# Windowed attention and a residual MLP on one core: a written-out instruction order replaced by a list scheduler, sink values taken through TensorE

## Chip, core and metric

One core of a Trainium2 chip runs the whole program. The metric is the device time of one execution in microseconds (us), from three runs of the kernel before.

## What is computed

Attention with 4 sink keys and a window of 128 keys over 4 batches of 8 heads, 768 positions and 64 dims; its output is the input of a token-mixing and channel-mixing MLP.

```python
keep = (pos_k < 4) | ((pos_q - pos_k >= 0) & (pos_q - pos_k < 128))
a = softmax(where(keep, q @ k.T / 8, -1e9));  x = (a @ v) as (B, 768, 512)
tok = einsum('ts,bsd->btd', w_tok, alpha1 * x + beta1)
u = x + lam * tok
ch = maximum((alpha2 * u + beta2) @ w_ch1, 0) @ w_ch2      # 512 -> 2048 -> 512
out = u + lam * ch
```

## The kernel before

The 768 positions are six blocks of 128. Per batch, eight tiles of q and k (`nat`, two heads each) are loaded, cast to fp16 (`n`), transposed by six TensorE transposes into `tp` and copied to `qkT` (line 210 is the copy helper on VectorE and GpSimd, line 208 on ScalarE). `scores` (lines 257 to 284) makes a block of scores in PSUM tile `S`, and ScalarE's exp turns it into `E`; `mask` multiplies it by a band mask (in batch 0 the mask is a bias added by TensorE instead). `pv` (293 to 313) multiplies E with the values `vf`, plus the sinks' part `es` with `vs`; `norm` (315 to 332) divides into `x` and makes `xh`, alpha1 times x, with GpSimd. `vs` holds the 4 sink rows of v spread over all partitions: four loads a batch (`load_vs`, line 77), and a GpSimd multiply with the mask `bm` (`fill_vs`, line 225).

The MLP of a batch: `tok` (six groups of 6 matmuls, line 382), the residual add on VectorE (389), a ScalarE cast `u` (391), transposes `uTp` to `uT` (404, 409), `h` (32 groups of 4 matmuls, 424) with relu on ScalarE or VectorE to `hT` (432, 430), `ch` (6 tiles of 16 matmuls, 444), add (450) and store (451). Weights are loaded once: w_tok is cast with row sums (472), transposed (475) and copied; w_ch1 is cast in quarters of 1 MB (`cast_w1`), w_ch2 is multiplied by lam in quarters (`cast_w2`, 487), through two 1 MB staging buffers `wst`.

Nothing reorders at run time: each engine runs its own instructions in the order in which the Python code issues them, and all loads and stores stand in SP's queue in one order. Before, that order is written by hand: lines 494 to 566 for attention of batch 0 and its token mixing, and from 569 on a list of `slots` (the MLP of batch b) with a `side` list of steps of attention b + 1 hung between them at computed positions. The loads of q, k, v of the next batch are issued together (`prefetch`, 613). In batch 0:

```python
side[6].append(lambda nb=nb: prefetch(nb))
side[12].append(lambda: (cast_w1(3, (A, G_)), load_w2(1)))
side[23].append(lambda: (cast_w2(1, (V, G_, V, G_)), load_w2(3)))
```

Of the kernel before, what the change touches and what calls it, by code (L numbers as in the profile page):

```python
# [10 lines left out]
ALU = mybir.AluOpType  # L11


@with_exitstack
def kernel(
# [17 lines left out]
    nc = tc.nc  # L33
# [22 lines left out]


    nat_tiles = {}
    v_tiles = {}

    def load_qk(b, hp, t):
        nat = sb.tile([P, 2, NR * D], FP32, tag="nat", bufs=8, name=f"nat{b}_{hp}_{t}")
        src = (q, k)[t][b, 2 * hp : 2 * hp + 2]
        nc.sync.dma_start(nat, src.rearrange("h (p r) d -> p h (r d)", p=P))
        nat_tiles[b, hp, t] = nat

    def load_v(b, r):
        vn = sb.tile([P, H, D], FP32, tag="vnat", bufs=4, name=f"vnat{b}_{r}")
        nc.sync.dma_start(vn, v[b, :, r * P : (r + 1) * P, :].rearrange("h p d -> p h d"))
        v_tiles[b, r] = vn  # L70

    vsn = {}

    def load_vs(b):
        vsn[b] = sb.tile([P, H, D], FP32, tag="vsn", bufs=1, name=f"vsn{b}")
        for i in range(n_sink):
            nc.sync.dma_start(
                vsn[b][i::n_sink], v[b, :, i, :].unsqueeze(0).to_broadcast([P // n_sink, H, D]))

    QK_ORDER = [(hp, t) for hp in range(HP) for t in range(2)]  # L80
# [75 lines left out]
    nc.vector.memset(bm, 1.0)  # L156

    for m in (maskn, mask0):
# [20 lines left out]
    )  # L179
    bias0 = const.tile([P, 1, 2 * P], FP16, name="bias0")  # L180
# [23 lines left out]
    xh_t = {}

    def copy(eng, o, i):
        if eng is nc.scalar:
            eng.copy(o, i)
        else:
            eng.tensor_copy(o, i)  # L210

    def cast_qk(b, hp, t, eng):
        nat = nat_tiles.pop((b, hp, t))
        d = sb.tile([P, NR, P], FP16, tag="n16", bufs=4, name=f"n16_{b}_{hp}_{t}")
        copy(eng, d.rearrange("p r (e d) -> p e r d", e=2), nat.rearrange("p e (r d) -> p e r d", r=NR))
        n16[b, hp, t] = d

    def cast_v(b, r, eng):
        copy(eng, vf[r][:, :, 0:D], v_tiles.pop((b, r)))

    def cast_v0(G, r, eng):
        copy(eng, vf[r][:, 4 * G : 4 * G + 4, 0:D], v0[G][:, r])

    def fill_vs(b):
        nc.gpsimd.tensor_mul(vs[b % 2][:, :, 0:D], vsn.pop(b), bmf.to_broadcast([P, H, D]))

    def trans(b, hp, t, eng=None):
        if b not in qkT:
            qkT[b] = sb.tile([P, 2 * HP, S], FP16, tag="qkT", bufs=1, name=f"qkT{b}")
        src = n16.pop((b, hp, t))  # L230
        pt = ps.tile([P, S], FP16, tag="d", bufs=3, name=f"tp{b}_{hp}_{t}")
        o = qkT[b][:, 2 * hp + t, :]
        for r in range(NR):
            nc.tensor.transpose(pt[:, r * P : (r + 1) * P], src[:, r, :], iden)  # L234
        copy(eng or nc.vector, o.rearrange("p (i r) -> p i r", r=NR),
             pt.rearrange("p (r i) -> p i r", r=NR))

    def sinks(b, Gs=(0, 1)):
# [3 lines left out]
        for e in range(2):  # L242
            nc.vector.tensor_copy(
                ks[64 * e : 64 * e + 64, hs, e * n_sink : (e + 1) * n_sink],
                qkT[b].rearrange("p (a t) s -> p a t s", t=2)[64 * e : 64 * e + 64, hs, 1, 0:n_sink],
            )
        pt = ps.tile([P, S - 2 * P], FP32, tag="d", bufs=3, name=f"sk{b}_{Gs[0]}")
        for hp in range(hs.start, hs.stop):
            nc.tensor.matmul(
                pt[32 * hp : 32 * hp + 32, :], ks[:, hp, :], qkT[b][:, 2 * hp, 2 * P : S],  # L250
                start=True, stop=True,
            )
# [410 lines left out]
```

## Time and profile before

| | us |
|---|---|
| median of 3 runs (range) | 337.0 (335.55 to 338.72) |
| profiled execution | 335.56 |
| its span, first to last instruction | 333.8 |
| PE busy, share of the span | 275.8, 83% |
| VectorE (DVE), ScalarE (ACT), GpSimd (POOL) busy | 167.0, 113.9, 118.8 |

PE is TensorE's matmul, PEld its weight load, SPq the queue in which SP issues DMAs. PEclk is TensorE's granted clock, 1.0 for 2.4 GHz and 0.5 for 1.2 GHz. Matmuls overlap and their ends are modelled, so a busy PE is not one at its peak. The span and the profiled execution's time differ by 1.8 us.

### The profile page before, as it was taken

What the parts mean: (1) busy time and instruction counts of PE and PEld (TensorE: products, weight loads), DVE (VectorE), ACT (ScalarE), POOL (GpSimd) and SP (SyncE); (2) the same over time, 40 slices, a digit from 0 to 9 for tenths busy, and PEclk for the clock granted to TensorE, in tenths of its full rate; (3) what the DMA queues carried; (4) which work ended last, traced back from release to release, by engine and by line L of the source; (5) the groups of instructions that cost most, each with busy time, mean ns of one, the idle gap of its engine ahead of it and who ended that gap; (6) DMA issues with size and microseconds to landing.
All of it is one profiled execution on the core that took longest, in us unless ns stands there. A gap on an engine that the chain in (4) does not pass through costs nothing.

```text
span 333.8 us, 4946 instructions
## 1 busy us (share of the span) xinstructions
PE 275.8 (83%) x1980; PEld 145.0 (43%) x1980; DVE 167.0 (50%) x325; ACT 113.9 (34%) x182; POOL 118.8 (36%) x138
## 2 busy tenths in 40 slices
PE   1775565789805888899999999999999999999995
PEld 1341222445403334445645455455554454566442
DVE  3362243552608887638836453388373634632211
ACT  3536313157200444103377420132765101445000
POOL 4484251002609936574403534453035350000000
PEclk9999567699975999999999999999999999999999
DMA  7899503037996205972000029940000111000021
GB/s 225 239 256 358 150 3 126 0 84 274 353 262 212 45 32 171 312 213 64 2 0 2 0 85 340 229 136 0 2 2 1 64 65 63 2 0 0 33 93 64
DMA packets 48166, 38.06 MB, mean 114 GB/s; under 512 B 31632, under 2 KB 39824, under 8 KB 48144
## 3 DMA queue, kind: packets, MB, share of 16 engines
q1 hardware_dynamic: 48144, 37.76, 36.8%
q8 instruction: 15, 0.25, 0.3%
q14 instruction: 7, 0.06, 0.1%
HBM read 31.46 MB, written 6.29 MB: 113 GB/s over the span
## 4 chain that ended last, share of the span: by engine, by line
PE 56%; DVE 20%; issue 8%; ACT 5%; POOL 5%; SPq 3%; DMA 2%; DVEq 0%; POOLq 0%; ACTq 0%
PE ch L444 22%; PE h L424 15%; PE tok L382 7%; DVE qkT L210 5%; DVE x L389 3%; DVE E L289 3%; PE S L271 3%; DVE uT L409 2%; DVE x L323 2%; POOL n L210 2%; ACT E L278 2%; ACT wt L472 2%; DMA wst_w<-in_moe_w_ch_dram 2%; SPq L96 2%; PE pv L310 1%
## 5 line engine op out<-in xcount | busy, mean ns | idle before, releaser
L424 PE MATMUL h<-uT,w1f 128*128 128x384 f16 x512 | 94.1, 330 | 2.7 <-ACT hT L432 1.4
L444 PE MATMUL ch<-w2f,hT 128*128 128x512 f16 x384 | 89.0, 379 | 0.0
L424 PEld LDWEIGHTS <-w1f 128*128 128x128 f16 x512 | 48.0, 99 | 35.6 <-issue 8.0
L432 ACT ACTIVATE hT<-h 128x384 f16<-128x384 f32 x88 | 42.7, 493 | 60.3 <-PE h L424 59.3
L444 PEld LDWEIGHTS <-hT 128*128 128x128 f16 x384 | 35.1, 98 | 38.4 <-issue 1.3
L278 ACT ACTIVATE E<-S 128x1024 f16<-128x1024 f32 (+1 forms) x42 | 40.4, 1003 | 29.0 <-PE S L271 29.0
L331 POOL TENSOR_TENSOR tmp<-x,la_b 128x512 f32<-128x512 f32 x18 | 22.8, 1269 | 74.4 <-DVE x L323 74.4
L391 ACT CAST u<-x 128x512 f16<-128x512 f32 x24 | 14.9, 620 | 82.4 <-DVE x L389 79.4
L430 DVE TENSOR_SCALAR hT<-h 128x384 f16<-128x384 f32 x40 | 22.2, 556 | 41.1 <-PE h L424 41.1
L450 DVE TENSOR_TENSOR x<-x,ch 128x512 f32<-128x512 f32 x24 | 16.5, 687 | 46.7 <-PE ch L444 46.7
L234 PE MATMUL tp<-iden,n 128*128 128x128 f16 x192 | 18.3, 239 | 24.7 <-POOL n L210 16.9
L382 PE MATMUL tok<-xh,wtokT 128*128 128x512 f16 x144 | 36.7, 409 | 0.7 <-DVE uT L409 0.6
L210 DVE COPY qkT<-tp 128x768 f16<-128x768 f16 x30 | 28.4, 953 | 10.5 <-PE tp L234 10.4
L210 POOL CAST n<-nat 128x768 f16<-128x768 f32 x29 | 24.4, 859 | 19.0 <-issue 12.9
L234 PEld LDWEIGHTS <-n 128*128 128x128 f16 x192 | 14.2, 107 | 31.4 <-POOL n L210 18.9
L332 POOL TENSOR_TENSOR xh<-tmp,lb_b 128x512 f16<-128x512 f32 x18 | 23.5, 1305 | 1.4
L382 PEld LDWEIGHTS <-wtokT 128*128 128x128 f16 x144 | 14.5, 104 | 18.0 <-issue 3.6
L389 DVE TENSOR_TENSOR x<-x,tok 128x512 f32<-128x512 f32 x24 | 16.5, 688 | 10.8 <-PE tok L382 10.2
L323 DVE TENSOR_TENSOR x<-pv,rec 128x256 f32<-128x256 f32 x48 | 20.4, 425 | 1.7
L289 DVE TENSOR_TENSOR E<-E,maskn 128x1024 f16<-128x1024 f16 x24 | 18.5, 772 | 1.4 <-ACT E L278 1.4
L487 POOL TENSOR_TENSOR w2f<-wst_w,lam_b 128x512 f16<-128x512 f32 x8 | 11.8, 1496 | 15.4 <-DMA wst_w<-in_moe_w_ch_dram 15.4
L306 PE MATMUL pv<-vf,E 128*128 128x65 f16 x160 | 15.7, 197 | 1.5 <-DVE x L323 1.2
(64 smaller groups left out, 226.1 us busy)
## 6 DMA issues: line engine op xcount, KB each, us to landing
wst_w<-in_moe_w_ch_dram SPq DMA_DIRECT2D x8, 1024.0 KB, 5.5
nat<-in_q_dram SPq DMA_DIRECT2D x16, 384.0 KB, 6.2
nat<-in_k_dram SPq DMA_DIRECT2D x16, 384.0 KB, 6.7
out_dram<-x SPq DMA_DIRECT2D x24, 256.0 KB, 2.0
vnat<-in_v_dram SPq DMA_DIRECT2D x18, 256.0 KB, 6.2
wtn<-in_moe_w_tok_dram SPq DMA_DIRECT2D x6, 384.0 KB, 7.6
v<-in_v_dram SPq DMA_DIRECT2D x12, 128.0 KB, 6.1
vsn<-in_v_dram SPq DMA_DIRECT2D x16, 64.0 KB, 3.1
```

The lines of the kernel that those rows point to most:

```text
L210: eng.tensor_copy(o, i)
L234: nc.tensor.transpose(pt[:, r * P : (r + 1) * P], src[:, r, :], iden)
L278: nc.scalar.activation(eT, pS, AF.Exp, scale=scale)
L289: nc.vector.tensor_mul(ev, ev, m.to_broadcast(list(ev.shape)))
L323: nc.vector.tensor_mul(x[:, 4 * G : 4 * G + 4, :], po[:, :, 0:D], rec.to_broadcast([P, 4, D]))
L331: nc.gpsimd.tensor_mul(tmp, xf, la1_b)
L332: nc.gpsimd.tensor_add(xh_t[b, r], tmp, lb1_b)
L382: nc.tensor.matmul(pt, wtokT[:, si, ti * P : (ti + 1) * P], xh_t[b, si], start=(si == 0), stop=(si == NR - 1),)
L389: nc.vector.tensor_add(xf, xf, pt)
L424: nc.tensor.matmul(ph, w1f[:, c, fi * P : (fi + 1) * P], uT[0][:, c, chk * NTOK : (chk + 1) * NTOK], start=(c == 0), stop=(c == NC - 1),)
L432: nc.scalar.activation(hT[chk][:, fi, :], ph, AF.Relu)
L444: nc.tensor.matmul(pch[ti], hT[chk][:, fi, nt * P : (nt + 1) * P], w2f[:, fi, :], start=(fi == 0), stop=(fi == NF - 1),)
```

## The change

The order is no longer written by hand. Each step becomes a task with a priority, the engines that may run it with a guessed cost in ns, the tasks it needs and the buffers it uses. `emit` repeatedly takes the task that can start first by its own bookkeeping (ties by priority), chooses the engine, hands it a buffer and issues it. The order is fixed when the kernel is built.

```diff
+    def emit(self):
...
+        while done < len(self.tasks):
+            best = None
+            for r, t in open_:
+                at = t.ready
...
+                for e in t.engs:
+                    key = (max(free[e], at), r, free[e] + t.engs[e])
+                    if best is None or key < best[0]:
+                        best = (key, t, e)
...
+            if e == SP:
+                channel = max(channel, free[e] + 1500.0) + t.lands
+                t.seen = channel + 300.0
+            else:
+                t.seen = free[e] + SEEN[e]
...
-    def fill_vs(b):
-        nc.gpsimd.tensor_mul(vs[b % 2][:, :, 0:D], vsn.pop(b), bmf.to_broadcast([P, H, D]))
+        def mm(e):
+            nc.tensor.matmul(pt.t, sel, vf[0][:, :, 0:D], start=True, stop=True)
+
+        def ev(e):
+            nc.vector.tensor_mul(vs[:, :, 0:D], pt.t, bmf.to_broadcast([P, H, D]))
...
+            done["xh", b, r, G] = add(p + 8.2, {POOL: 730, DVE: 420}, half, [a, done["la1"]], [bx, bh])
...
+            done["w1", i, c] = add(
+                p, {ACT: 600, POOL: 645, DVE: 330},
...
+            done["w2", 4 * i + a] = add(
+                p, {DVE: 900, POOL: 1400},
...
+        done["h", b, chk, fi] = add(p + 0.1, {ACT: 493, DVE: 556}, relu, [a], [ph, bh])
...
+    nc.scalar.dma_start(alpha2_c, moe_alpha2.rearrange("(c p) -> p c", p=P))
+    nc.scalar.dma_start(beta2_c, moe_beta2.rearrange("(c p) -> p c", p=P))
...
+        for i in range(4):
+            load_w2(at(), i)
...
+            pl = w0 - (0 if b == 0 else 30)
+            for i, (hp, t) in enumerate(QK_ORDER):
+                load_qk(pl + 0.5 * i, nb, hp, t)
```

- Sink rows: the 16 loads are gone. `sel`, a 128x128 fp16 matrix of ones and zeros made at the start, picks the first 4 rows of `vf` in one 512-column matmul per batch, and VectorE multiplies PSUM by `bm`. There is one `vs` buffer where there were two.
- PSUM: `pv` had a bank of its own and all else three; now all share four.
- The loads of alpha2 and beta2 (512 elements each) go from SP's queue to the front of ScalarE's.
- Casts of w_ch1 are four per quarter instead of two, on any of three engines; products of w_ch2 go to VectorE or GpSimd as `emit` finds them; so do the relus of h (ScalarE or VectorE) and batch 0's halves of xh.
- Two `ch` tiles are now filled in turns, 4 matmuls each.

ScalarE, from the end of attention of batch 0 to the token mixing (`E0` exp, `wt16` cast of w_tok, `u16` cast after tok). Before:

```order
L278 ACTIVATE E0_5_1_541<-S0_5_1_534 128x512
L472 ACTIVATE wt16_2_543,rs_71<-wtn0_109 128x768
L208 CAST w1f_165<-wst_w1_0_113 128x2x512
L391 CAST u16_0_0_597<-x0_0_244 128x512
L472 ACTIVATE wt16_3_599,rs_71<-wtn1_115 128x768
L391 CAST u16_0_1_618<-x0_1_270 128x512
L472 ACTIVATE wt16_4_620,rs_71<-wtn1_115 128x768
L391 CAST u16_0_2_639<-x0_2_306 128x512
L472 ACTIVATE wt16_5_641,rs_71<-wtn1_115 128x768
```

And now:

```order
L461 ACTIVATE E0_5_1_592<-S0_5_1_565 128x512
L563 ACTIVATE wt16_3_612,rs_71<-wtn1_263 128x768
L563 ACTIVATE wt16_4_626,rs_71<-wtn1_263 128x768
L204 COPY wtokT_119<-wT3_628 128x6x128
L204 COPY wtokT_119<-wT4_644 128x6x128
L563 ACTIVATE wt16_5_674,rs_71<-wtn1_263 128x768
L204 COPY wtokT_119<-wT5_690 128x6x128
L204 CAST u16_0_0_715<-x0_0_246 128x512
L204 CAST u16_0_1_728<-x0_1_299 128x512
```

The casts 3 to 5 of w_tok stood behind the casts of u that follow a tok; they now stand ahead of all of them.

SP's queue around the second quarter of w_ch2 (`wst_w2_1`; the digit in `nat1`, `vnat2` is the batch). Before:

```order
L64 DMA nat1_3_1_787<-in_k_dram 128x2x384
L69 DMA vnat1_0_789<-in_v_dram 128x8x64
L69 DMA vnat1_1_791<-in_v_dram 128x8x64
L69 DMA vnat1_2_793<-in_v_dram 128x8x64
L69 DMA vnat1_3_795<-in_v_dram 128x8x64
L77 DMA vsn1_797<-in_v_dram 32x8x64 x4
L110 DMA wst_w2_1_840<-in_moe_w_ch2_dram 128x4x512
```

And now:

```order
L331 DMA wst_w1_3_753<-in_moe_w_ch1_dram 128x4x512
L300 DMA vnat1_4_758<-in_v_dram 128x8x64
L300 DMA vnat1_5_775<-in_v_dram 128x8x64
L300 DMA vnat2_0_789<-in_v_dram 128x8x64
L300 DMA vnat2_1_808<-in_v_dram 128x8x64
L294 DMA nat2_3_1_819<-in_k_dram 128x2x384
L331 DMA wst_w2_0_857<-in_moe_w_ch2_dram 128x4x512
L294 DMA nat3_0_0_868<-in_q_dram 128x2x384
L294 DMA nat3_0_1_950<-in_k_dram 128x2x384
L294 DMA nat3_1_0_962<-in_q_dram 128x2x384
L331 DMA wst_w2_1_982<-in_moe_w_ch2_dram 128x4x512
```

Before, the eight loads of q and k of batch 1 and these of v stood between w2_0 and w2_1. Now they stand ahead of most weights, and loads of batches 2 and 3 stand among the quarters.

VectorE around the products of w_ch2 (`w2f`) in batch 0. Before:

```order
L210 COPY qkT1_908<-tp1_0_1_925 128x768
L430 TENSOR_SCALAR hT0_1_750<-h0_1_11_933 128x384
L487 TENSOR_TENSOR w2f_166<-wst_w2_1_840,lam_b_66 128x512 x2
L210 COPY qkT1_908<-tp1_1_0_947 128x768
L210 COPY qkT1_908<-tp1_1_1_966 128x768
L210 COPY qkT1_908<-tp1_2_0_985 128x768
```

And now:

```order
L470 TENSOR_TENSOR E1_0_1_1040<-E1_0_1_1040,mask0_79 128x1024
L417 TENSOR_TENSOR vs_117<-vsp1_1038,bm_85 128x8x64
L591 TENSOR_TENSOR w2f_121<-wst_w2_0_857,lam_b_66 128x512 x2
L470 TENSOR_TENSOR E1_1_0_1072<-E1_1_0_1072,maskn_80 128x1024
L470 TENSOR_TENSOR E1_1_1_1082<-E1_1_1_1082,maskn_80 128x1024
L516 RECIPROCAL rec1_0_0_1130<-pv1_0_0_1084 128x4
```

The products of w2_1 stood ahead of six of the eight qkT copies of batch 1; all eight now come before the first product, and the products stand between the masks.

## Rows read from the trace of the kernel before

**Rows 1.** TensorE's granted clock in 40 equal slices of the span

```profile
PEclk9999567699975999999999999999999999999999
```

**Rows 2.** Windows by stage: us, busy time of each engine, PEclk, DMA share, GB/s

```profile
25.70:45.10 19.40, 11.36 (x108) 5.47 (x108) 5.56 (x17) 9.61 (x14) 6.11 (x11) 0.72 0.61 205
45.10:68.40 23.30, 14.75 (x70) 6.81 (x68) 11.63 (x20) 5.05 (x11) 5.42 (x5) 0.72 0.12 45
68.40:92.00 23.60, 20.39 (x141) 12.13 (x139) 11.31 (x18) 12.30 (x23) 7.54 (x7) 1.00 0.81 253
92.00:114.80 22.80, 9.14 (x61) 5.46 (x62) 12.31 (x15) 2.99 (x6) 15.04 (x16) 0.70 0.67 188
114.80:146.90 32.10, 28.46 (x234) 13.33 (x233) 22.30 (x42) 10.32 (x12) 19.65 (x17) 1.00 0.55 166
212.90:278.80 65.90, 63.23 (x481) 34.01 (x480) 37.40 (x75) 24.77 (x40) 22.91 (x23) 1.00 0.17 52
278.80:333.80 55.00, 51.10 (x285) 26.64 (x282) 17.73 (x31) 14.31 (x28) 0.00 (x0) 1.00 0.09 34
```

**Rows 3.** Timeline of one round of token mixing, batch 0: start, us, engine, line

```profile
55.79 0.62 ACT L391 CAST u<-x 128x512 f16<-128x512 f32 x1 [4.00 <-DVE x L389]
56.32 0.84 ACT L472 ACTIVATE wt<-wtn 128x768 f16<-128x768 f32 x1
...
57.30 0.51 PE L475 MATMUL wT<-iden,wt 128*128 128x128 f16 x6 [2.27 <-ACT wt L472]
57.65 2.30 PE L382 MATMUL tok<-xh,wtokT 128*128 128x512 f16 x6
...
61.23 0.84 ACT L472 ACTIVATE wt<-wtn 128x768 f16<-128x768 f32 x1
```

**Rows 4.** Timeline, 80 to 105 us: SP's queue, then GpSimd, VectorE, TensorE

```profile
83.09 7.80 SPq L69 DMA_DIRECT2D vnat<-in_v_dram  x4
...
94.17 9.41 SPq L110 DMA_DIRECT2D wst_w<-in_moe_w_ch_dram  x3
...
82.13 2.49 POOL L487 TENSOR_TENSOR w2f<-wst_w,lam_b 128x512 f16<-128x512 f32 x2 [4.25 <-DMA wst_w<-in_moe_w_ch_dram]
...
99.76 3.43 POOL L487 TENSOR_TENSOR w2f<-wst_w,lam_b 128x512 f16<-128x512 f32 x2 [11.13 <-DMA wst_w<-in_moe_w_ch_dram]
...
99.71 2.36 DVE L487 TENSOR_TENSOR w2f<-wst_w,lam_b 128x512 f16<-128x512 f32 x2 [9.88 <-DMA wst_w<-in_moe_w_ch_dram]
...
104.01 0.82 PE L234 MATMUL tp<-iden,n 128*128 128x128 f16 x6 [12.40 <-POOL n L210]
```

**Rows 5.** Chain that ended last, its two longest pieces: start, us, what

```profile
291.66 17.70 PE h L424 x108
309.36 20.73 PE ch L444 x96
```

**Rows 6.** Groups by line: xcount | busy us, mean ns | idle before

```profile
L278 ACT ACTIVATE E<-S 128x1024 f16<-128x1024 f32 x40 | 39.2, 1023 | 25.1 <-PE S L271 25.1
...
L332 POOL TENSOR_TENSOR xh<-tmp,lb_b 128x512 f16<-128x512 f32 x18 | 23.5, 1305 | 1.4
...
L289 DVE TENSOR_TENSOR E<-E,maskn 128x1024 f16<-128x1024 f16 x24 | 18.5, 772 | 1.4 <-ACT E L278 1.4
...
L487 POOL TENSOR_TENSOR w2f<-wst_w,lam_b 128x512 f16<-128x512 f32 x8 | 11.8, 1496 | 15.4 <-DMA wst_w<-in_moe_w_ch_dram 15.4
...
L210 POOL CAST vf<-vnat 128x512 f16<-128x512 f32 x18 | 11.3, 643 | 0.0
L487 DVE TENSOR_TENSOR w2f<-wst_w,lam_b 128x512 f16<-128x512 f32 x8 | 9.9, 1279 | 9.9 <-DMA wst_w<-in_moe_w_ch_dram 9.9
```

**Rows 7.** Timeline of the start, SP's queue and ScalarE

```profile
9.34 3.44 SPq L77 DMA_DIRECT2D vsn<-in_v_dram  x4
...
5.05 0.83 ACT L208 CAST n<-nat 128x768 f16<-128x768 f32 x1 [2.97 <-DMA nat<-in_k_dram]
```

**Rows 8.** Window of 2 us in the loads of q and k, columns as in rows 2

```profile
84.00:86.00 2.00, 1.93 (x16) 1.04 (x15) 1.86 (x3) 0.49 (x1) 2.00 (x3) 1.00 1.07 400
```

More of the change, by code (lines that the diff above doesn't have):

```diff
@@ L1 @@
+import bisect
 from contextlib import ExitStack
@@ L11, with __init__ @@
 ALU = mybir.AluOpType
+PE, ACT, DVE, POOL, SP = "pe", "act", "dve", "pool", "sp"
+SEEN = {PE: 200, ACT: 60, DVE: 60, POOL: 70}
+class Buf:
+    def __init__(self, kind, shape, dtype, name):
+        self.kind, self.shape, self.dtype, self.name = kind, shape, dtype, name
+        self.left = 0
+        self.freed = 0.0
+        self.home = None
+        self.t = None
+class Task:
+    def __init__(self, prio, engs, fn, after, uses, mode, lands):
+        self.prio, self.engs, self.fn, self.uses = prio, engs, fn, uses
+        self.mode, self.lands = mode, lands
+        self.needs = [a for a in after if a is not None and a.seen is None]
+        self.ready = max([0.0] + [a.seen for a in after if a is not None and a.seen is not None])
+        self.then = []
+        self.seen = None
@@ L55, with copy @@
     ctx.enter_context(tc.manual_schedule())
[L58 to L80, printed above, removed]
+    engine = {ACT: nc.scalar, DVE: nc.vector, POOL: nc.gpsimd}
+    pools = {
+        "nat": (sb, [P, 2, NR * D], FP32),
+        "vnat": (sb, [P, H, D], FP32),
+        "n16": (sb, [P, NR, P], FP16),
+        "qkT": (sb, [P, 2 * HP, S], FP16),
+        "E": (sb, [P, 2, 2, 2 * P], FP16),
+        "es": (sb, [P, S - 2 * P], FP16),
+        "x": (sb, [P, H, D], FP32),
+        "xh": (sb, [P, DM], FP16),
+        "tmp": (sb, [P, DM], FP32),
+        "rec": (sb, [P, 4, 1], FP32),
+        "u16": (sb, [P, DM], FP16),
+        "uT": (sb, [P, NC, S], FP16),
+        "hT": (sb, [P, NF, NTOK], FP16),
+        "wst": (sb, [P, 4, 512], FP32),
+        "d": (ps, [P, 512], FP32),
+        "S": (ps, [P, 2, 512], FP32),
+    }
+    homes = {
+        "nat": 8, "vnat": 4, "n16": 4, "qkT": 1, "E": 6, "es": 1, "x": 12, "xh": 6, "tmp": 2,
+        "rec": 2, "u16": 4, "uT": 1, "hT": 2, "wst": 2, "d": 4, "S": 2,
+    }
+    plan = Plan(pools, homes)
+    add = plan.add
+    def copy(e, o, i):
+        if e == ACT:
+            nc.scalar.copy(o, i)
+        else:
+            engine[e].tensor_copy(o, i)
     lam_b = const.tile([P, DM], FP32, name="lam_b")
@@ L156 @@
     nc.vector.memset(bm, 1.0)
-    for m in (maskn, mask0):
+    sel = const.tile([P, P], FP16, name="sel")
+    nc.vector.memset(sel, 0.0)
+    for m in (mask0, maskn):
         nc.gpsimd.affine_select(
@@ L239, in sinks @@
+    def sinks(p, b, Gs=(0, 1)):
         n = len(Gs)
@@ L241, in sinks @@
         g = slice(64 * Gs[0], 64 * Gs[0] + 64 * n)
[L242 to L252, printed above, removed]
@@ new lines, in mlp2, with mm, oa @@
+    def mlp2(p, b, ti, part):
+        chk, nt = ti // 3, ti % 3
+        if part == 0:
+            pch[b, ti] = Buf("d", None, None, f"ch{b}_{ti}")
+        pc, bh, bx = pch[b, ti], hT[b, chk], x[b, ti]
+        fis = range(4 * part, 4 * part + 4)
+        def mm(e):
+            for fi in fis:
+                nc.tensor.matmul(
+                    pc.t, bh.t[:, fi, nt * P : (nt + 1) * P], w2f[:, fi, :],
+                    start=(fi == 0), stop=(fi == NF - 1))
+        a = done["ch", b, ti] = add(
+            p, {PE: 4 * 214}, mm,
+            [done["h", b, chk, fi] for fi in fis] + [done["w2", fi] for fi in fis]
+            + [done.get(("ch", b, ti))], [pc, bh])
+        if part == 3:
+            def oa(e):
+                xf = bx.t.rearrange("p h d -> p (h d)")
+                nc.vector.tensor_add(xf, xf, pc.t)
+            a = add(p + 0.1, {DVE: 690}, oa, [a, done["u16", b, ti]], [pc, bx])
+            add(p + 0.2, {SP: 480}, lambda e: nc.sync.dma_start(
+                out[b, ti * P : (ti + 1) * P, :], bx.t.rearrange("p h d -> p (h d)")),
+                [a], [bx], lands=800)
@@ new lines, with at @@
+    t0 = -1000.0
+    n = 0
+    def at():
+        nonlocal n
+        n += 1
+        return t0 + 0.5 * n
+    for hp, t in QK_ORDER[:4]:
+        load_qk(at(), 0, hp, t)
+    for r in range(2):
+        load_v0(at(), 0, r)
+    load_const(at(), "lam", lam_b, moe_lam)
+    load_const(at(), "a1", la1_b, moe_alpha1)
+    for r in range(2, NR):
+        load_v0(at(), 0, r)
+    for hp, t in QK_ORDER[4:]:
+        load_qk(at(), 0, hp, t)
+    for r in range(NR):
+        load_v0(at(), 1, r)
+    for ti in range(3):
+        load_wtok(at(), ti)
@@ new lines @@
+    for i, (hp, t) in enumerate(QK_ORDER):
+        g = -950 + 5 * i if i < 4 else -890 + 8 * (i - 4)
+        trans(g, 0, hp, t, ANY, {DVE: 955, ACT: 880}, cast_p=g - 20)
+    for G in range(2):
+        for r in range(NR):
+            cast_v0(-900 + 60 * G + 10 * r, G, r)
+    fill_vs(-890, 0)
+    for G in range(2):
+        base = -900 + 60 * G
+        for j in range(NR):
+            scores(base + 10 * j, 0, j, (G,), bias=True)
+            if j == 1:
+                sinks(base + 12, 0, (G,))
+        for r in range(NR):
+            pv(base + 10 * r + 14, 0, r, G)
@@ L456, in dense @@
+    for ti in range(NR):
+        cast_wtok(-800 + 8 * ti, ti)
+    cast_w1(-770, 0)
+    STEP = 100.0
+    for b in range(B):
+        w0 = STEP * b
         if b == 0:
+            seq = [("tok", ti) for ti in range(3)] + [("uT", 0, 0), ("uT", 0, 1)]
+            seq += [("tok", ti) for ti in range(3, NR)]
             m1 = []
@@ L561 @@
[L561 to L581 removed]
+                    m1 += [("m1", chk, fi) for fi in range(4 * qd, 4 * qd + 4)]
@@ new lines @@
+            m1.insert(3, ("uT", 1, 0))
+            m1.insert(5, ("uT", 1, 1))
+        else:
+            seq = [("tok", ti) for ti in range(5)] + [("uT", 0, 0), ("uT", 0, 1), ("tok", 5)]
+            m1 = [("m1", 0, fi) for fi in range(NF)]
+            m1.insert(4, ("uT", 1, 0))
+            m1.insert(6, ("uT", 1, 1))
+            m1 += [("m1", 1, fi) for fi in range(NF)]
+        seq += m1
+        seq += [("m2", ti, part) for ti in range(NR) for part in range(4)]
+        ns = len(seq)
+        if b == 0:
+            for i in range(1, 4):
+                cast_w1(w0 + 8 + 8 * (i - 1) - 4, i)
+            for i in range(4):
+                cast_w2(w0 + 26 + 4 * i, i)
```

817 lines of the change are left out of this document (420 added, 397 removed).

## Prediction

> **What bounds the kernel now.** I read the slices first, then windows cut at the stages, then the timeline inside the windows where TensorE is idle, and the groups by line last, for prices. The slices show TensorE at 2.4 GHz throughout the second half, and below it in two places in the first [rows 1]. The windows say why the halves differ [rows 2]. The last batch has no attention beside it and takes 55.0 us, 51.1 of them TensorE. A batch with the next one's attention beside it takes 65.9, of which TensorE is idle for 2.7. Batch 0 has no such rhythm: token mixing of batch 1 starts only at 146.9. Of the 66.3 us from 25.7 to 92 TensorE shows 46.5 busy, most of it at a mean clock of 0.72, and from 92 to 114.8 only 9.1 of 22.8. So this is a TensorE-bound kernel behind a front that is bound by waits, and the change has to earn its time in the front.
>
> Two kinds of wait are in that front. In token mixing each round is a loop over three engines: ScalarE casts u of the last tile, then casts a row of w_tok, TensorE transposes it after 2.27 us without a matmul, and only then comes the next tok [rows 3]. The casts of two rounds start at 56.32 and 61.23, so a round takes 4.9 us, for six matmuls. From 92 on, VectorE and GpSimd both sit at the product with the second quarter of w_ch2, for 9.88 and 11.13 us; its load was issued at 94.17, behind four loads of v that took SP's queue 7.80 us; and TensorE waits 12.40 us for a cast of n that stands behind GpSimd's product [rows 4].
>
> **The change part by part.** The sum is made against the profiled execution, 335.56, which is its span of 333.8 and 1.76 around it, and lies 1.4 under the median of the three runs.
>
> Start to the end of attention, batch 0. The four sink loads held SP's queue for 3.44 us at 9.34 [rows 7]; all loads behind them come that much earlier. The alpha2 and beta2 issues go ahead of ScalarE's first cast, which waited 2.97 us for its own load [rows 7]: I count nothing, and at most 2 us if two issues outlast that cover; the two short ops that make `sel` stand before GpSimd's first load in the same way. Before, the second half of the heads starts at 25.7 and token mixing at 45.1, and ScalarE is busy for 9.6 of these 19.4 us [rows 2], because each cast of w_tok, its transposes and the next scores wait for one another in turn. The new order gives ScalarE more: six exps (one of them half as long), one of the sinks (half), five w_tok casts (0.84 and the read of a row sum, 1.0) and four copies of the same shape (0.84), together 6 x 1.02 + 5 x 1.0 + 4 x 0.84 = 14.5 [rows 3, 6], with gaps 15, now without waiting in turn. It starts at about 23 (the first w_tok cast now stands ahead of the first of these exps and waits for its load, which eats half of the 3.4 us won). 23 + 15 = 38 for the start of token mixing, 7 us earlier. GpSimd's halves of xh end there too. One wait is new: the matmul with `sel` needs the first block of v for all heads, and pv of blocks 2 to 5 stand behind it on TensorE; that load is issued behind only four tiles of q and k (1 us each, [rows 8]) more than before's sink rows were, so I count nothing, at most 2.
>
> Token mixing, 45.1 to 68.4 before. The loop is cut: the casts of w_tok stand ahead of every cast of u. Left are 36 matmuls of 512 columns. The dense run of ch prices one at 20.73 / 96 = 0.216 us [rows 5], so 7.8 us at 2.4 GHz; as the stage before leaves TensorE half idle, I take the first two tiles at 1.2 GHz (+2.6), and 1.6 for the transposes. 38 + 12 = 50 for the first h; before it was 68.4. Lower bound 10, upper 18 (the clock low throughout, 16 + 2).
>
> h with attention of batch 1, 68.4 to 114.8 before: 46.4 us. h itself is 128 x 17.70 / 108 = 21.0 us [rows 5]. The eight tiles of transposes, five of six score blocks and some pv lie between, about 27,000 columns for a whole attention, three quarters of them here, at 0.216 per 512: 8.5 us. So 30, and 80 for the first ch. The 12.40 us go only if no load is late. Since w_ch2's quarters now stand behind loads of three batches, I follow the queue. At 400 GB/s [rows 8] a q or k tile takes 1.0 us and a quarter 2.6; v's 256-byte pieces are slower, between that and the 134 GB/s of 1 MB in 7.80 us behind a backlog [rows 4]; I take 270. Up to w1_1 the queue holds 13 MB by the tiles' sizes, which land by 43 at a mean 300; four of v and w1_2 by 50; seven of q and k, w1_3, four of v, one of k and w2_0 by 68; three more and w2_1 by 74; w2_2 by 80. VectorE wants w2_0 at about 72. These all come in time, by 3 to 5 us. w2_3 does not: its buffer is w2_1's, whose last product on GpSimd stands behind the first tmp of batch 1, so it is issued near 84, lands at 88 and is multiplied by 93, where TensorE wants it at 88. A stall of 5.
>
> ch with the rest of attention, 114.8 to 146.9 before: 32.1. Now 24 groups of 4 at 0.864 are 20.7, pv and scores 4, the stall 5: 30, which ends at 110. GpSimd agrees: from 69 on it has eight products of w_ch2 less those VectorE takes in both orders (8 x 1.496 stay), six pairs of tmp and xh (12 x 1.3) and six v casts (6 x 0.643), 31.4 us in all [rows 6], and most waits of it lie inside: 100 at the earliest, about 108 with them.
>
> Here the profile gives a lever against the change, since it adds VectorE work with two SBUF operands beside a GpSimd that is full. GpSimd's two products took 2.49 us with little beside them, and 3.43 beside VectorE's two, which took 2.36 [rows 4]: it lost 0.94, not 2.36. My 1.496 includes this. The Trainium skill (SBUF — State Buffer, section "SBUF: two separate sides") says that the pair of ports they share is an exclusive lock and the other engine blocks for the whole instruction. By that rule every mask and product of VectorE would stop GpSimd. The trace shows less than half of it.
>
> Steady batches, 65.9 each. TensorE's work hardly changes: four matmuls of 512 columns in all are added, 0.9 us. Visible idle is 2.7 [rows 2]; by columns the floor is 51.1 + 27,000 / 512 x 0.216 = 62.5, and 60.2 if score matmuls on the two halves of the rows overlap fully. New orders of tp, pv and ch can remove idle, and cannot remove columns. I take 63.6; bounds 60.2 and 67, one us above today: two ch tiles filled in turns hold two of the four shared PSUM banks, and a pv that finds none free stops the matmuls behind it until a norm. Sinks leave GpSimd; VectorE gets four products of 128x512, at most 1.279 each as for the same shape [rows 6], and it is busy for 37 of 66: nothing on the path.
>
> Last batch: same matmuls, same last add and store: 55.0.
>
> Sum: 110 + 2 x 63.6 + 55.0 = 292.2, and 1.8 around it, 294.0; with the 1.4 to the median, 295.
>
> **The rivals.** (1) Weights come late and replace the removed wait. For it: loads of batches 2 and 3 stand between the quarters, each waiting for a buffer that a cast must free, and casts wait for transposes. Against it: before, SP's queue waited on hand-placed issues, not on bytes. If w2_3's products end at 108, not 93: 295 + 15 = 310. (2) All goes well: no stall at w2_3 and no late load (104), batches at 60.5: 295 - 6 - 6 = 283. (3) VectorE and GpSimd exclude each other: ten masks of 0.772 and eight products of 1.279 [rows 6] fall into GpSimd's 31 us; that is 18, of which 1.496 holds about half, and of the other 9 a third finds GpSimd waiting anyway: 6 more, 301. This is the rule of the Trainium skill named above. (4) Slower: TensorE never gets its clock back in the front. The rows show it at 0.5 to 0.75 after thin stretches [rows 1, 2]. If scattered short waits kept it at 1.2 GHz from 38 to the end of ch, the 7.8 + 21 + 20.7 + 11 us of matmuls there would take twice as long, 60.5 more less the 2.6 counted already and the 5 of stall that it hides: 110 + 53 = 163 for batch 1, 348 in all. It decides from 41 us of doubled work on. Against it: from 68.4 to 92, with h alone, it was 1.00 [rows 2], and the new front is denser. (5) The change doesn't do what it says: the order rests on guessed costs, and the in-order queues give back as other waits what they save; the front stays at 147: 337.
>
> **How the numbers follow.** Forecast 0.58, (1) 0.16, (2) 0.10, (3) 0.10, (4) 0.04, (5) 0.02. The forecast's own error is some 8 us, from the stage bounds. The range runs from just under (2) to just past (1): 281 to 312. A run of this kernel scatters by about 1%, so faster means below 333.6 and slower above 340.4. Only (4) is slower, 0.04, and (5) the same, 0.02: faster has 0.94.
>
> **What would show it.** In the changed profile: the first tok near 38, the first h near 50, the first ch near 80, tok of batch 1 near 110; no wait of TensorE above 6 us after 30; a clock of 1.0 from about 45 on; then two batches of 63 to 64 and one of 55. A wait of VectorE or GpSimd on a `wst_w` load of over 8 us speaks for (1); GpSimd's tmp and xh well above 1.3 for (3); a low clock with TensorE busy for (4). The forecast is wrong if tok of batch 1 comes after 125, or if a steady batch takes more than 67.

## The result and the profile after

The changed kernel takes 292.33 us (median of 4 runs, 291.89 to 293.79) against 337.86 for the kernel before on the same chip: a ratio of 0.867, 95% interval 0.860 to 0.873, so 13% faster. 295.0 was predicted. The clock row and the windows of the profile after, cut at its own stages (attention of batch 0 with the transposes of w_tok; token mixing; h; ch; the two steady batches; the last batch), answer to [rows 1] and [rows 2], with the same columns:

```profile
PEclk9999789999799899999999999999999999999999
```

```profile
0.00:39.10 39.10, 25.78 (x269) 14.54 (x270) 26.58 (x68) 24.58 (x36) 22.69 (x39) 0.91 1.01 315
39.10:48.70 9.60, 9.60 (x70) 5.25 (x68) 8.63 (x14) 5.13 (x10) 7.76 (x12) 1.00 0.97 254
48.70:82.70 34.00, 28.83 (x231) 16.91 (x229) 25.01 (x38) 19.63 (x35) 16.38 (x16) 0.95 1.04 324
82.70:111.70 29.00, 25.31 (x174) 12.17 (x173) 20.86 (x35) 3.73 (x5) 25.87 (x21) 0.94 0.44 125
111.70:173.60 61.90, 61.62 (x482) 34.41 (x481) 37.99 (x76) 25.57 (x41) 25.89 (x26) 1.00 0.19 61
173.60:235.50 61.90, 61.62 (x482) 34.47 (x481) 37.97 (x76) 25.57 (x41) 19.04 (x16) 1.00 0.07 27
235.50:291.10 55.60, 51.78 (x289) 27.07 (x287) 20.45 (x37) 11.96 (x23) 0.00 (x0) 1.00 0.10 38
```

Batch 1's token mixing starts at 111.7 instead of 146.9: 35 of the 43 us that the span lost. The other 8 are two steady batches of 61.9 instead of 65.9, in which TensorE's visible idle time fell from 2.7 to 0.3 us. The last batch takes 0.6 more.

The DMA share (the last but one number) is about 1.0 up to 82.7, where [rows 2] had 0.12 to 0.81: the transfers now fill the front. That share alone doesn't say that they bind it (the start of a_pvbank, below, has 1.01 too and is 8.3 us longer), but the chain that ended last has loads in it, in pieces of seven to eleven microseconds (start, us, what):

```profile
22.28 11.37 DMA nat<-in_q_dram
33.73 10.04 DMA wst_w<-in_moe_w_ch_dram
44.60 7.21 DMA wst_w<-in_moe_w_ch_dram
...
64.08 7.43 DMA wst_w<-in_moe_w_ch_dram
```

The timeline of the place that [rows 4] showed before, w_ch2's arrival (start, us, engine, line, operation, and in brackets the idle time before it and what ended it):

```profile
52.92 9.90 SPq L300 DMA_DIRECT2D vnat<-in_v_dram  x4
...
64.08 0.37 SPq L331 DMA_DIRECT2D wst_w<-in_moe_w_ch_dram  x1
...
71.58 3.44 POOL L591 TENSOR_TENSOR w2f<-wst_w,lam_b 128x512 f16<-128x512 f32 x2 [6.53 <-DMA wst_w<-in_moe_w_ch_dram]
...
77.19 0.68 DVE L470 TENSOR_TENSOR E<-E,maskn 128x1024 f16<-128x1024 f16 x1
...
85.06 2.89 DVE L591 TENSOR_TENSOR w2f<-wst_w,lam_b 128x512 f16<-128x512 f32 x2
...
85.68 6.73 POOL L591 TENSOR_TENSOR w2f<-wst_w,lam_b 128x512 f16<-128x512 f32 x4
...
87.87 1.75 DVE L470 TENSOR_TENSOR E<-E,maskn 128x1024 f16<-128x1024 f16 x1
...
89.55 3.42 DVE L591 TENSOR_TENSOR w2f<-wst_w,lam_b 128x512 f16<-128x512 f32 x2
...
93.57 4.43 PE L693 MATMUL ch<-w2f,hT 128*128 128x512 f16 x12 [3.20 <-DVE x L517]
```

GpSimd still waits 6.53 us for the first quarter, issued at 64.08, after four v loads that held the queue for 9.90. From 77.3 to 93.6 VectorE is busy for 15.8 of 16.3 us and GpSimd for 16.2, and a norm that would free a PSUM buffer comes behind VectorE's products: TensorE waits 3.20 us for it. The 12.40 us wait is gone.

### The profile page after: what moved, and what is told of

Same layout as the page of the kernel before. It is cut to its first block, busy times and chain, and to the rows that moved or that the text cites. A ratio compares the mean times of both kernels' runs of the same rounds, so it can differ in the third digit from the quotient of the medians.

```text
span 291.1 us, 4977 instructions
## 1 busy us (share of the span) xinstructions
PE 264.5 (91%) x1984; PEld 144.8 (50%) x1984; DVE 177.5 (61%) x338; ACT 116.2 (40%) x189; POOL 117.6 (40%) x127
## 3 DMA queue, kind: packets, MB, share of 16 engines
q1 hardware_dynamic: 42736, 36.71, 40.2%
q10 hardware_dynamic: 1056, 0.00, 0.2%
## 4 chain that ended last, share of the span: by engine, by line
PE 66%; DMA 15%; DVE 11%; SPq 4%; issue 1%; POOL 1%; ACT 0%; ACTq 0%; DVEq 0%; POOLq 0%
PE ch L693 27%; PE h L669 25%; DMA wst_w<-in_moe_w_ch_dram 8%; PE tok L608 6%; DMA nat<-in_q_dram 4%; DVE w2f L591 4%; SPq L311 3%; PE pv L493 2%; DVE E L470 2%; PE S L448 2%; DMA beta_c<-in_moe_beta_dram 2%; SPq L294 1%; DMA v<-in_v_dram 1%; PE tp L367 1%; DVE qkT L206 1%; DVE uT L654 1%
## 5 line engine op out<-in xcount | busy, mean ns | idle before, releaser
L669 PE MATMUL h<-uT,w1f 128*128 128x384 f16 x512 | 92.9, 329 | 4.4 <-DVE x L517 3.0
L693 PE MATMUL ch<-w2f,hT 128*128 128x512 f16 x384 | 90.1, 384 | 3.7 <-DVE x L517 3.2
L693 PEld LDWEIGHTS <-hT 128*128 128x128 f16 x384 | 36.1, 99 | 45.2 <-DVE x L517 3.7
L534 POOL TENSOR_TENSOR tmp<-x,la_b 128x512 f32<-128x512 f32 x18 | 24.4, 1356 | 44.8 <-DVE x L517 44.5
L608 PE MATMUL tok<-xh,wtokT 128*128 128x512 f16 x144 | 33.7, 379 | 0.0
L206 DVE COPY qkT<-tp 128x768 f16<-128x768 f16 x28 | 26.6, 951 | 2.4 <-PE tp L367 2.3
L537 POOL TENSOR_TENSOR xh<-tmp,lb_b 128x512 f16<-128x512 f32 x18 | 24.7, 1374 | 0.9
L470 DVE TENSOR_TENSOR E<-E,maskn 128x1024 f16<-128x1024 f16 x24 | 21.9, 918 | 4.5 <-ACT E L461 4.5
L493 PEld LDWEIGHTS <-E 128*128 128x128 f16 x328 | 16.3, 99 | 9.0 <-issue 2.9
L493 PE MATMUL pv<-vf,E 128*128 128x65 f16 x328 | 19.0, 196 | 1.3 <-ACT E L461 1.3
```

The source lines that it names most:

```text
L206: engine[e].tensor_copy(o, i)
L470: nc.vector.tensor_mul(ev, ev, m.to_broadcast(list(ev.shape)))
L493: nc.tensor.matmul(po.t[:, hl, :], eT.t[:, e_, off + i, c : c + P], vf[j][:, h, :], start=(r < 2 and n == 0), stop=(n == len(parts) - 1 an ...
L534: nc.gpsimd.tensor_mul(tmp.t, bx.t.rearrange("p h d -> p (h d)"), la1_b)
L537: nc.gpsimd.tensor_add(bh.t, tmp.t, lb1_b)
L608: nc.tensor.matmul(pt.t, wtokT[:, si, ti * P : (ti + 1) * P], hs[si].t, start=(si == 0), stop=(si == NR - 1))
```

## The experiments

The kernel before was timed beside each run (337.3 to 337.5). Stage starts are the starts of the first tok, h and ch on TensorE.

**One part alone, in the order by hand.** b_sinks takes only the sinks through TensorE:

```diff
-        nc.gpsimd.tensor_mul(vs[b % 2][:, :, 0:D], vsn.pop(b), bmf.to_broadcast([P, H, D]))
+        nc.tensor.matmul(pt[:, hs], sel, vf[0][:, hs, 0:D], start=True, stop=True)
+        nc.vector.tensor_mul(vs[b % 2][:, hs, 0:D], pt[:, hs], bmf[:, hs].to_broadcast([P, n, D]))
```

> The kernel before with its hand-written order; only the sink values are taken through TensorE (a matmul with the selection matrix and a VectorE product; for batch 0 once per half of the heads) and the 16 sink loads are gone. Theory (order, not sinks, makes the gain): 2 to 5 us off 337.9, because SP's queue loses 3.44 us of issues per batch, of which only those between 84 and 105 us stand in front of something that is waited for. Rival (the small sink loads were what clogged the queue): 12 us or more off, with the first tok of batch 1 at 135 or earlier instead of 146.8.

334.97 us, ratio 0.992 (0.988 to 0.996): 2.6 us, as the theory had it. TensorE still waits 11.5 us for the cast of n behind the second quarter's product.

b_loop moves three calls:

```diff
     pvn0(4, 1)
+    cast_wtok(3, V)
     pvn0(5, 1)
+    cast_wtok(4, V)
+    cast_wtok(5, V)
...
     tok[0]()
-    cast_wtok(3, V)
     tok[1]()
-    cast_wtok(4, V)
     tok[2]()
-    cast_wtok(5, V)
```

> The kernel before; only the casts and transposes of the last three rows of w_tok are moved ahead of the first tok, so that no cast of u stands in front of one. Theory (the loop over ScalarE, TensorE and VectorE sets token mixing): from the first tok to the first h 13 us instead of 23.3, some 2 to 3 us later start of tok, and the whole 6 to 9 us shorter. Rival (TensorE's half clock sets that stage, whatever the order): the stage stays above 19 us and the gain is under 3.

328.15 us, ratio 0.973 (0.967 to 0.979), 9.1 us less. Its window of token mixing is 15.0 long where [rows 2] had 23.3, and it starts 0.7 us earlier, not 2 to 3 later. The clock is still 0.77 (0.72 before), so the cut loop made most of the 8.3 us:

```profile
44.40:59.40 15.00, 11.90 (x52) 5.30 (x50) 10.39 (x17) 2.80 (x5) 5.14 (x5) 0.77 0.20 70
```

b_queue issues v and the sinks of batch 1 behind the second quarter of w_ch2:

```diff
-                for r in range(4):
-                    load_v(bb, r)
-                load_vs(bb)
+                if bb > 1:
+                    prefetch_v(bb)
...
+                side[12].append(lambda nb=nb: prefetch_v(nb))
```

> The kernel before; only the loads of v and of the sinks for batch 1 are issued after the second quarter of w_ch2 instead of ahead of it (the tiles of q and k stay where they are). Theory (the order in SP's queue makes the 12.40 us wait of TensorE): the waits of 9.88 and 11.13 us on that quarter shrink below 3, the whole is 7 to 11 us shorter. Rival (too many bytes, whatever their order): the wait moves to the cast of v or to the third quarter and the gain is under 3 us.

333.25 us, ratio 0.989 (0.983 to 0.994): 3.9 us, between the two. The waits are a third to a half of [rows 4], not below 3: the order was half of it. What is left I put down to bytes, which no run here tests by itself. The quarter is issued at 84.69 rather than 94.17, but lands only at 94; the eight tiles of q and k (3.1 MB) are issued just ahead of it, and from 84 to 94 the DMA engines move 391 GB/s.

```profile
84.69 0.37 SPq L110 DMA_DIRECT2D wst_w<-in_moe_w_ch_dram  x1
...
86.06 1.93 DVE L487 TENSOR_TENSOR w2f<-wst_w,lam_b 128x512 f16<-128x512 f32 x2
...
94.20 3.43 POOL L487 TENSOR_TENSOR w2f<-wst_w,lam_b 128x512 f16<-128x512 f32 x2 [3.99 <-DMA wst_w<-in_moe_w_ch_dram]
...
98.46 0.82 PE L234 MATMUL tp<-iden,n 128*128 128x128 f16 x6 [5.98 <-POOL n L210]
```

b_all has all three edits.

> The three edits of the other runs together, by hand, on the kernel before. Theory: they add up, 16 to 24 us off, with tok of batch 1 at 122 to 130; what is then missing to 292.3 (20 to 28 us) lies in the start (6), in the h and ch stage of batch 0 beside the attention of batch 1 (6 to 10), and in the two steady batches (4 each). Rival (only an order that is packed as a whole gets the gain, since each wait removed by hand comes back as the next one): under 12 us.

322.95 us, ratio 0.958 (0.954 to 0.963). By the ratios the three parts nearly add up (15.6 us one by one, 14.0 together), so the rival falls, but so does the size that was expected, and tok of batch 1 starts at 134.8. Span against span, 31.2 us are missing to the changed kernel: 9.1 until the first tok (48.2 against 39.1), 5.3 in token mixing, 6.1 in h, 2.6 in ch, 8.5 in the steady batches, less 0.4 in the last.

**One part taken out of the changed kernel.** a_sinkloads brings the loads back:

```diff
-            nc.tensor.matmul(pt.t, sel, vf[0][:, :, 0:D], start=True, stop=True)
+                nc.sync.dma_start(
+                    bf.t[i::n_sink], v[b, :, i, :].unsqueeze(0).to_broadcast([P // n_sink, H, D]))
```

> The changed kernel with the sink values loaded again (four loads per batch, GpSimd's product into vs) and planned by the same scheduler. Theory (the order makes the gain): 1 to 4 us above 292.3, from 3.44 us more of SP's queue in the start and one GpSimd product more per batch where GpSimd is full, 25.9 of the 29.0 us from 82.7 to 111.7. Rival (the sinks through TensorE carry a good part of the gain in this packed order): 8 us or more above.

296.99 us, ratio 0.880 (0.876 to 0.883): 4.7 us above, just past the theory's end. The first tok comes 3.1 us later, about the queue's 3.44, and tok of batch 1 6.7 later. In the order by hand the same part was worth 2.6; that a front full of loads feels SP's queue more is my reading, which no run isolates.

a_fixed binds every step to the engine that it had before:

```diff
-                p, {DVE: 900, POOL: 1400},
+                p, {POOL: 1400} if a % 2 else {DVE: 900},
-        done["h", b, chk, fi] = add(p + 0.1, {ACT: 493, DVE: 556}, relu, [a], [ph, bh])
+        done["h", b, chk, fi] = add(p + 0.1, {DVE: 556} if fi % 3 == 2 else {ACT: 493}, relu, [a], [ph, bh])
```

> The changed kernel without the elastic choice of engine: each cast, copy, half of xh, relu and product of weights is bound to the engine that it had before; order, buffers and sinks as the scheduler makes them. Theory (order, not choice of engine): 0 to 5 us above 292.3, all of it ahead of batch 1. Rival (the choice of engine carries the front): 10 us or more above, with the first tok at 44 or later.

294.38 us, ratio 0.871 (0.867 to 0.875), whose interval overlaps that of the changed kernel. So the choice of engine is worth at most a few microseconds. They are not where I expected them: tok of batch 1 starts at 111.9, as with the choice, and the steady batches take 62.5 instead of 61.9.

a_ab puts alpha2 and beta2 back into SP's queue, behind w_tok:

```diff
-    nc.scalar.dma_start(alpha2_c, moe_alpha2.rearrange("(c p) -> p c", p=P))
-    nc.scalar.dma_start(beta2_c, moe_beta2.rearrange("(c p) -> p c", p=P))
...
+        done[nm] = add(at(), {SP: 500}, lambda e, tl=tl, ap=ap: nc.sync.dma_start(
+            tl, ap.rearrange("(c p) -> p c", p=P)), lands=800)
```

> The changed kernel with the loads of alpha2 and beta2 back in SP's queue, behind the rows of w_tok. Prediction's step (they cost nothing where they are, since ScalarE waits for its first tile anyway): within 0.5 us of 292.3, the first tok at 39. Theory now (their 1024 four-byte packets delay the first tiles; ScalarE's first cast began at 6.28, not at 5.05, and TensorE at 5.32, not at 4.56): 0.8 to 1.5 us less, the first tok at 38.

292.2 us, ratio 0.865 (0.861 to 0.868): no difference, so the second theory falls for the whole. The first microseconds do move. TensorE's first transposes, of the changed kernel and then of a_ab, each with ScalarE's first cast:

```profile
5.32 0.82 PE L367 MATMUL tp<-iden,n 128*128 128x128 f16 x6 [5.32 <-DVE n L206]
...
6.28 0.83 ACT L204 CAST n<-nat 128x768 f16<-128x768 f32 x1 [3.12 <-DMA nat<-in_k_dram]
```

```profile
4.46 0.82 PE L365 MATMUL tp<-iden,n 128*128 128x128 f16 x6 [4.46 <-DVE n L206]
...
5.02 0.83 ACT L204 CAST n<-nat 128x768 f16<-128x768 f32 x1 [2.94 <-DMA nat<-in_k_dram]
```

The first tok, though, came at 40.2 in a_ab and 39.1 in the changed kernel; the 0.86 us don't reach it.

a_pvbank divides PSUM as before:

```diff
-        "rec": 2, "u16": 4, "uT": 1, "hT": 2, "wst": 2, "d": 4, "S": 2,
+        "rec": 2, "u16": 4, "uT": 1, "hT": 2, "wst": 2, "d": 3, "pv": 1, "S": 2,
```

> The changed kernel with PSUM divided as before: three shared buffers, and one of its own for pv, so that the planner can't give pv's bank to h, tok or the transposes, nor two banks to pv. Theory (the 4 us that a steady batch gained, 65.9 to 61.9, come from the pooled fourth bank): 64 to 66 us for each of the two steady batches, 4 to 10 us above 292.3 in all. Rival (they come from the order alone): batches at 62 to 63, within 2 us of 292.3.

300.69 us, ratio 0.890 (0.886 to 0.894): 8.4 above, a size that the theory gave, at a place that it did not. The windows of the start and of the steady batches:

```profile
0.00:47.40 47.40, 29.43 (x275) 16.29 (x276) 30.11 (x75) 25.05 (x37) 27.92 (x44) 0.87 1.01 299
...
120.10:180.30 60.20, 59.46 (x447) 32.20 (x447) 36.41 (x73) 24.69 (x39) 24.32 (x24) 1.00 0.17 55
180.30:244.00 63.70, 62.85 (x483) 34.39 (x482) 40.66 (x79) 24.20 (x38) 18.52 (x16) 1.00 0.07 26
```

The steady batches take 62.0 on the mean, as with the pooled bank, so what they won isn't the bank's. The start takes 8.3 more. The edit also makes the scheduler plan another order, so the 8.3 are the worth of the bank with the order that it allows. TensorE's waits from 20 to 48 us name two places (in total, times, longest): pv, with one bank, waits 4.8 for norms, and the transposes of w_tok wait 4.5 for a VectorE copy, which I read as the one that empties one of the three shared banks.

```profile
PE wT L570 <- DVE qkT L207: 4.5, 1, 4.5
PE pv L494 <- DVE x L518: 3.4, 2, 2.5
PE pv L487 <- DVE x L518: 1.4, 2, 0.7
```

The changed kernel has neither wait there; its longest up to the first tok is:

```profile
PE tp L367 <- POOL n L206: 3.1, 1, 3.1
```

**What holds the front now.** Either the order of the loads or the weight products: two theories, each with an edit. a_w2act lightens the products on VectorE and GpSimd (w_ch2 and lam are rounded to fp16 ahead of the product too, not only behind it):

```diff
-            done["w2", 4 * i + a] = add(
-                p, {DVE: 900, POOL: 1400},
-                lambda e, a=a: engine[e].tensor_mul(w2f[:, 4 * i + a, :], src.t[:, a, :], lam_b),
+            c = add(p, {ACT: 620}, lambda e, a=a: nc.scalar.copy(w2f[:, 4 * i + a, :], src.t[:, a, :]),
...
+                lambda e, a=a: nc.vector.tensor_mul(w2f[:, 4 * i + a, :], w2f[:, 4 * i + a, :], lam16),
```

> The changed kernel, in which w_ch2 is cast to fp16 by ScalarE and then multiplied by an fp16 copy of lam in place on VectorE, so that GpSimd has no product of weights and VectorE's have two bytes an element. Theory (from 72 to 97 us VectorE and GpSimd, both full with these products in fp32 beside each other, set the pace of TensorE, and GpSimd again to 111.7): 4 to 9 us below 292.3, with the first ch at 76 to 81 and tok of batch 1 at 103 to 108. Rival (the loads of the quarters, or the PSUM buffers and ScalarE's relus, set it): within 2 us, or slower, because ScalarE gets 16 casts of 0.62 us.

289.0 us, ratio 0.856 (0.853 to 0.860), 3.3 less, under the theory's 4. ch takes 24.7 instead of 29.0 and h 33.0 instead of 34.0: most of the gain lies in ch.

a_late loads batches 2 and 3 behind the weights; the new dependency serves the planner alone, so only the order changes:

```diff
+        late = [done["wst", "w2_3"]] if b > 1 else []
...
-            uses=[bf], lands=1030)
+            late, uses=[bf], lands=1030)
```

> The changed kernel, in which the loads of q, k and v of batches 2 and 3 are planned after the load of the last quarter of w_ch2 (before, eight tiles of batch 2 stood ahead of the last quarter of w_ch1 in SP's queue and eleven of batches 2 and 3 between that and the second quarter of w_ch2). Theory A (bytes loaded too soon delay the weights: GpSimd waited 6.53 us for the first quarter of w_ch2 at 71.58): 2 to 5 us below 292.3, the longest wait on a weight under 2. Theory B (the products on VectorE and GpSimd set the pace from 72 on, whenever the quarters land): within 1.5 us.

288.91 us, ratio 0.855 (0.850 to 0.859): 3.4 less, so theory B falls and the size is theory A's. GpSimd's longest wait for a quarter of w_ch2 is 2.2 where it was 6.53. But the gain doesn't lie where that wait was: the first ch starts at 82.6, where it started at 82.7. The first quarter lands at 59.5 instead of 71.5 and the last product ends at 82.0 instead of 93.0, so none is left beside ch, which takes 25.0 instead of 29.0. That is the same 4 us which the lighter products gave.

a_w2act_late has the edits of both.

> Both edits together: products of w_ch2 by ScalarE's cast and VectorE's fp16 product, and the loads of batches 2 and 3 behind the weights. Theory (with the products light, what is left in the h stage is ScalarE's wait for the first quarters, behind which relus queue, 2.67 us of TensorE at 74.75): 2 to 5 us below the 289.0 of the first edit alone, tok of batch 1 at 103 to 106. Rival (the low clock after any gap and the PSUM buffers eat it): within 1.5 us of 289.0.

288.53 us, ratio 0.853 (0.849 to 0.858): the rival's size. h now takes 30.4, but ch 28.0. The four products of the last quarter, which take 0.42 us each where GpSimd is idle, take 4.37 beside GpSimd's xh and casts of n; a norm stands behind them, and TensorE waits 2.55 for it:

```profile
77.25 4.37 DVE L595 TENSOR_TENSOR w2f<-w2f,lam 128x512 f16<-128x512 f16 x4
...
82.22 0.40 PE L488 MATMUL pv<-vs,es 128*128 128x260 f16 x1 [2.55 <-DVE x L519]
```

The windows around that wait:

```profile
70.00:82.00 12.00, 7.72 (x69) 4.33 (x67) 11.85 (x21) 10.16 (x17) 7.07 (x6) 1.00 1.06 366
82.00:90.00 8.00, 7.78 (x56) 4.05 (x57) 6.45 (x12) 1.54 (x2) 6.42 (x6) 0.79 1.22 291
```

a_w2mix_late leaves every fourth product on GpSimd:

```diff
+            if a == 3:
+                done["w2", 4 * i + a] = add(
+                    p, {POOL: 1400},
```

> The changed kernel with the loads of batches 2 and 3 behind the weights, and of the four products of each quarter of w_ch2 three by ScalarE's cast and VectorE's fp16 product, the fourth by GpSimd in fp32. Theory (what is left from 70 to 82 is VectorE, 11.85 of 12.0 us busy with both edits, while GpSimd has 7.07): 1 to 2 us below the 288.5 of both edits. Rival (the rest lies in the order and in the clock that falls after each gap, not in one engine's load): within 0.7 us of 288.5.

283.48 us (282.58 to 284.52, 6 runs), ratio 0.840 (0.836 to 0.844), 5.0 less, more than either theory gave, and the fastest version: 3% below the changed kernel. The same windows, and the same place:

```profile
70.00:82.00 12.00, 10.98 (x100) 6.13 (x99) 11.73 (x24) 9.92 (x17) 8.77 (x8) 1.00 1.09 368
82.00:90.00 8.00, 8.00 (x64) 3.89 (x63) 7.89 (x12) 2.61 (x3) 7.79 (x7) 1.00 1.05 237
```

```profile
77.81 2.96 DVE L601 TENSOR_TENSOR w2f<-w2f,lam 128x512 f16<-128x512 f16 x3
...
81.38 1.90 PE L703 MATMUL ch<-w2f,hT 128*128 128x512 f16 x8 [0.45 <-DVE x L519]
```

VectorE is as full as in a_w2act_late (11.73 of 12.0 us), so its load, which I had priced, isn't what changed; as far as these lines show, it is what stands ahead of the norm. TensorE is busy 3.3 us longer in the first window, and in the second its clock stays at 1.00 instead of 0.79, which is worth 1.7 us of 8 by my estimate: together the 5.0. The steady batches stay at 61.9; h and ch together take 53.4 us, where the prediction's column prices give 21 + 8.5 + 20.7 + 4 = 54.

## Why the prediction was right, step by step

**Start, 38 (39.1 measured).** The number held, the reason only in part. I took ScalarE's order as the cause and put the pooled PSUM bank at nothing here. a_pvbank is planned by the same scheduler without that bank and starts tok at 47.4, no earlier than before: 8.3 us hang on the bank. Nor is ScalarE full from 23 on, as 14.5 us of work in 15 had it. It is busy for 12.1 of the 16.1 us to the first tok and waits 3.89 for transposes of w_tok, and TensorE waits 3.07 for GpSimd's cast of batch 1's n:

```profile
34.68 0.82 PE L367 MATMUL tp<-iden,n 128*128 128x128 f16 x6 [3.07 <-POOL n L206]
...
37.06 1.50 ACT L204 COPY wtokT<-wT 128x768 f16<-128x768 f16 x2 [3.89 <-PE wT L569]
```

**Loads of alpha2 and beta2, nothing.** Right for the whole (a_ab), though the first transposes move by 0.86 us.

**Sinks, 3.4 us off SP's queue, half of it at the first tok.** Right in kind, too small: a_sinkloads loses 3.1 at the first tok. In all the sinks are worth 2.6 (b_sinks) or 4.7 (a_sinkloads).

**Token mixing, 12 (9.6).** The mechanism held (b_loop). I put two tiles at the low clock; the clock was 1.00, and the stage came out under my lower bound of 10.

**h and ch, 30 and 30 (34.0 and 29.0).** The term for h was 4 too small. One step that failed in size is "These all come in time, by 3 to 5 us": the first quarter of w_ch2 landed at 71.5, not 68, and GpSimd waited 6.53 us for it. That wait alone isn't the 4 us, as a_late removes it and the first ch stays at 82.6. TensorE's longest wait in h is for a norm that stands behind two products and two masks of VectorE, all slower beside GpSimd:

```profile
71.53 2.37 DVE L591 TENSOR_TENSOR w2f<-wst_w,lam_b 128x512 f16<-128x512 f32 x2 [2.08 <-DMA wst_w<-in_moe_w_ch_dram]
...
73.82 2.35 DVE L470 TENSOR_TENSOR E<-E,maskn 128x1024 f16<-128x1024 f16 x2
...
76.78 2.72 PE L669 MATMUL h<-uT,w1f 128*128 128x384 f16 x8 [3.01 <-DVE x L517]
```

With earlier loads h takes 32.8, with light products 33.0, with both 30.4. The stall I did forecast in ch, of 5 for a product of the last quarter, came as 0.5 for a product and 3.20 for a norm behind such products, at 93.57; those products ended at 92.4 and 93.0, where I had 93.

**The lever against the change.** The step "less than half of it" was a wrong reading of [rows 4]. I compared the 0.94 us that GpSimd lost with the 2.36 of VectorE's two products, but the 2.36 held waits too. With GpSimd idle, as from 93.4 to 95.7 in a_pvbank, such a product takes 0.68:

```profile
93.91 0.68 DVE L592 TENSOR_TENSOR w2f<-wst_w,lam_b 128x512 f16<-128x512 f32 x1
```

So 0.94 is some two thirds of what VectorE's two need. The changed kernel shows the same. GpSimd's four products from 85.68 take 6.73 us, 1.68 each, and beside each of them stands one product or mask of VectorE, which would take 0.68 alone. A GpSimd product takes 1.25 with little beside it [rows 4]. Without contention a pair would take 1.25, by turns 1.93: again some two thirds of the way to turns. The mask's mean rose with it, beside 0.772 in [rows 6]:

```profile
L470 DVE TENSOR_TENSOR E<-E,maskn 128x1024 f16<-128x1024 f16 x24 | 21.9, 918 | 4.5 <-ACT E L461 4.5
```

The Trainium skill's rule of an exclusive lock (SBUF — State Buffer, "SBUF: two separate sides") describes these microseconds better than my reading of [rows 4] did, though not fully: by it a pair would have taken 1.93, an estimate from the rows above. GpSimd's tmp and xh, 1.3 before, take 1.64 to 1.72 from 77.35 to 94.05, the sign that I had named for rival (3).

**Steady batches, 63.6 (61.9).** Inside the bounds, 1.7 too high for each. Removing idle time was the mechanism, 2.4 of the 4.0 us by the windows; without the bank they take 62.0 on the mean, with loaded sinks 60.5 and 61.7, with fixed engines 62.5, so by exclusion it is the order, the two ch tiles in turns included, which no run takes out alone. How the other 1.6 came off, within matmuls whose ends are modelled, stays open.

**Last batch, 55.0 (55.6).** Right.

The misses nearly cancel: 111.7 for tok of batch 1 against 110, and 3.4 saved in the steady batches. Of the 2.7 us between 295 and 292.3, 1.9 are only that I added 1.4 from the profiled run to the median, where the changed kernel's profiled run (292.78) lies 0.45 above its median. So the closeness of the sum is in part luck. Of the rivals, (1) and (3) each name something real. Earlier loads are worth 3.4 us, not 15; lighter products, which relieve the contention of (3) but are also less work, 3.3; the TensorE clock of (4) stayed at 0.91 to 1.00 in every stage; (5) falls with the result.

## What to carry to other kernels

Split the gain before crediting one idea: the loop cut by hand gave 9 us, the load order 4, the sinks 3 to 5, one pooled PSUM bank with the order that it allows 8, and the choice of engine about nothing that the runs can tell. When a front becomes dense, look next at what is prefetched ahead of the bytes that are waited for, and at what stands ahead of an instruction that frees PSUM; earlier loads or lighter products alone gave 3 us, and both, with a quarter of the products left on GpSimd, 9. A planner guesses landing times: one added dependency made the first quarter land 12 us earlier (a_late), so read in the trace where its in-order queues wait for loads.

## What was not expected of the hardware

An fp16 product of 128x512 in place on VectorE took 0.42 us where GpSimd was idle (three at 72.76 in a_w2act) and the fp32 one 0.68. Beside GpSimd's xh and casts of n the fp16 product took 1.04 to 1.48 (four at 77.25 in a_w2act_late), no less than the fp32 one beside such casts (two in 1.93, b_queue at 86.06). And two small loads of 1056 packets in all, with 5.16 us to the landing of the second, put off the first transposes of a program by 0.86 us although they carry 4 KB (a_ab).
